# The age at which a unit's gate matmuls enter the program order: from over 13 to over 17

## The chip, the cores and the metric

The kernel runs on one core of one Trainium2 chip. The metric is the device time of one execution in microseconds (us). A core has TensorE (matmuls; the profile calls it PE, and PEld for its weight loads), VectorE (DVE), ScalarE (ACT), GpSimd (POOL, which here only issues indirect DMAs after the first few hundred microseconds) and SyncE (SP, which issues the other DMAs). Each engine works through its own instructions in the order of the program and waits on semaphores for the others.

## The reference

A causal convolution with 7 taps, whose taps are a softmax over each head's weights, makes 28672 tokens of 192 values. A gate then picks two of eight experts for each token, and the output is the weighted sum of the two experts' results:

```python
logits = x @ w_gate
noise_scale = np.log1p(np.exp(x @ w_noise))
noisy_logits = logits + noise_scale * noise
top2 = np.argpartition(-noisy_logits, 2, axis=1)[:, :2]
...                                   # top2_w: softmax over the two
for e in range(E):
    h = np.maximum(x[mask] @ w1[e], 0.0)          # 192 -> 1024
    out[mask] += top2_w[mask, k, None] * (h @ w2[e])   # 1024 -> 192
```

Here E = 8, and mask holds the tokens that have expert e as their k-th choice.

## The kernel before

**Two streams of work.** The tokens are cut into 28 units of 1024 (128 partitions by 8). A unit is convolved on DVE (`conv`, lines L411, L413: 56 instructions), scaled and split into two f16 halves in one of two buffers `rb` (ACT at L443 and L444, then DVE at L446 and L448), routed (`gating`), and its rows are written to a table `xs` in DRAM, ordered by expert (`scatter`, L567: 16 indirect DMAs on POOL for a unit). The experts work on that table in 29 rounds of 8 blocks, one block for each expert; a block has 256 rows of the table (128 in round 0). Round r, from round 9 on, needs the rows of unit r + 1 and all before it; rounds 0 to 8 need unit r.

**A block.** `load_block` loads a block's rows transposed (`bT`, SP, L688), two blocks ahead, into one of three buffers. `mm1` (L654) runs the first matrix in two halves of 20 matmuls; after each half ACT takes the ReLU (L657) and DVE what f16 left of it (L658). `mm2` (L668) runs the second matrix, 48 matmuls, one block late; ACT scales the two results (L671), and POOL adds them to the output with two indirect DMAs (L672). The order on PE is: first half of block n, `mm2` of block n-1, second half of block n. At the first block of a round SP also loads the rows' tokens and weights (`mt`, L594), and DVE makes the round's indices of them (`round_meta`, L613 to L634).

**Slots.** After each half of a block's first matrix the order has a slot: slot 2n after the first half of block n (k = 0), slot 2n + 1 after the second (k = 1). In a slot `Side.slot` first lets `pace` put one or more scatters into POOL's order, then `route` may put in some steps of one unit's routing, and then `convolve` puts in convolution work while a credit lasts. The order on PE, DVE, ACT and SP is that of the program.

**Routing of a unit** has these steps. The *first part* (age set to 0) issues on SP the unit's noise load, a store of zeros to the output and eight DMA transposes of `rb` into `xT` (L472; for units from 3 on). The *second step* puts in the 40 gate matmuls (L481), the reading of their result (L496 to L498) and an exponential (L500). Then come, each in a later slot with k = 0, log1p (L502 to L512) and the choice of two (L519 to L533), and at the next k = 1 the ranks (PE, L538 and L541), the rows' places (L545 to L563), and the 16 scatters join the queue that `pace` empties. Only now counts the unit as routed (`gate_done`).

**What couples them.** Each slot with 256 rows adds 4.05 to the age and 5.0 (k = 0) or 1.4 (k = 1) to the convolution's credit, times a rate of 0.7 where two more units are routed than the next five rounds need, or 1.0. Routing steps take from the same credit (4.1 for log1p, 3.1 for the choice, 2.8 for the places). A unit's convolution starts only when the unit two before it is routed; with it go the copy of the halo (ACT, L373) and the load of the next unit's input (L179). The ACT instruction that writes `rb` for unit u is put in once the queue holds no scatter of unit u - 2, and when it runs it waits for those scatters' DMAs to have read the buffer:

```python
while queue and queue[0][0] <= u - NRB:
    yield 0.0, True
rb = rbs[u % NRB]
nc.scalar.activation(rb[:, :, 0:128], xc[:, :, 0:128], AF.Copy)
```

`pace` takes 2 and 1 scatters in turn at each slot, or more where the round that needs them is near.

Of the kernel before, what the change touches and what calls it, by code (L numbers as in the profile page):

```python
# [32 lines left out]
def kernel(  # L33
# [305 lines left out]
    NRB, NPE = 2, 3  # L339
    rbs = []  # L340
    for i in range(NRB):
        rb = rpool.tile([P, TU, ROW], F16, name=f"rb{i}")
        V.memset(rb[:, :, 384:ROW], 0.0)
        rbs.append(rb)
    NPART = U // 2 if U % 2 == 0 else U
    nzt, route, cps = {}, {}, {}
    scat, zeroed = {}, []

# [396 lines left out]
    class Side:  # L745
# [11 lines left out]
        def route(self, k):  # L757
            if self.b is None:
                if self.gate_u <= self.conv_done and self.gate_u < U:
                    self.b, self.step, self.age = gating(self.gate_u), 0, 0.0  # L760
                    self.run_b(1)
            elif self.step == 1:
                if k == 0 and self.age > (4.0 if self.gate_u < NPE else 13.0):
                    self.run_b(3)
            elif self.step < 4:
                if k == 0:
                    self.run_b(1)
            elif k == 1:
                self.run_b(3)
                self.b = None  # L770
                self.gate_done = self.gate_u
                self.gate_u += 1
# [156 lines left out]
```

## Time and profile before

| | |
|---|---|
| three executions, median (lowest, highest) | 2248.9 us (2246.77, 2252.76) |
| the profiled execution, its own time | 2245.47 us |
| its span, first to last instruction | 2243.1 us |
| mean granted TensorE clock | 0.965 |
| PE / PEld / DVE / ACT / POOL busy, share of the span | 92% / 85% / 68% / 35% / 60% |

All numbers of the trace are of the one profiled execution. Its own time is 2.4 us above its span and 3.4 us below the median. In a listing of instructions a row has the start and the length in us, the engine, the line, the operation, what it writes and reads, and in brackets the idle time of the engine before it and what ended it. A row of a table by stretches has the bounds and the length in us, then the busy time and number of instructions of PE, PEld, DVE, ACT and POOL, the granted clock of TensorE (1.00 is full), the DMA engines' share and GB/s. A row of the waits reads "who <- what it waited for: us in total, times, longest".

### The profile page before, as it was taken

How to read it: one execution, taken by the hardware profiler on the slowest of the kernel's cores; microseconds unless marked ns; L12 is line 12 of the kernel's file. 1: busy time of each engine (PE TensorE's matmuls, PEld its weight loads, DVE VectorE, ACT ScalarE, POOL GpSimd, SP SyncE). 2: the span in 40 equal slices, each digit the busy share in tenths (PEclk: the TensorE clock that was granted, in tenths of full speed). 3: DMA queues.
4: the chain of work that ended last, by engine and by line, in shares of the span. 5: the costliest groups of instructions: out<-in, count | busy, mean ns of one | idle time of the engine just before them, and what ended most of it. 6: DMA issues, size and time to landing. Idle time of an engine off the chain costs nothing.

```text
span 2243.1 us, 53253 instructions
## 1 busy us (share of the span) xinstructions
PE 2059.7 (92%) x22126; PEld 1915.9 (85%) x22126; DVE 1523.4 (68%) x4009; ACT 795.1 (35%) x1168; POOL 1336.4 (60%) x923
## 2 busy tenths in 40 slices
PE   6569686999799999999999999999999999999997
PEld 5568585889698888899999989999999999999997
DVE  6468674788687878777778777787778875423332
ACT  5354231333233333333333333333333333333332
POOL 0463544676675676677666766667666666543333
PEclk8789797999999999999999999999999999999999
DMA  8524454565556657656556665666655665443332
GB/s 232 169 55 71 99 84 101 109 107 109 111 104 105 108 98 110 115 117 117 91 90 110 118 111 84 101 112 119 119 86 97 106 108 102 70 58 50 51 50 32
DMA packets 462774, 223.66 MB, mean 100 GB/s; under 512 B 342152, under 2 KB 449720, under 8 KB 462393
## 3 DMA queue, kind: packets, MB, share of 16 engines
q1 hardware_dynamic: 375352, 129.38, 28.6%
q0 software_dynamic: 87168, 90.76, 26.6%
q8 instruction: 175, 2.87, 0.5%
q14 instruction: 79, 0.65, 0.1%
HBM read 40.12 MB, written 115.38 MB: 69 GB/s over the span
## 4 chain that ended last, share of the span: by engine, by line
PE 68%; DVE 7%; SPq 5%; issue 4%; DMA 3%; another core or an unknown queue 3%; ACT 2%; POOL 1%; POOLq 0%; DVEq 0%; ACTq 0%
PE ph L654 34%; PE py L668 33%; SPq L472 5%; DVE h L658 3%; ACT h L657 2%; DMA xT<-rb 1%; DVE xc L413 1%; PE misc L481 1%; DMA bT<-xs 1%; POOL out_dram L672 1%; DMA out_dram<-y,ids 1%; POOL xs L567 1%; DVE xc L411 1%; ACT y L671 0%
## 5 line engine op out<-in xcount | busy, mean ns | idle before, releaser
L672 POOL DMA_INDIRECT out_dram<-y,ids x456 | 792.9, 1739 | 553.9 <-ACT y L671 338.8
L654 PE MATMUL ph<-bT,w1s 128*128 128x256 f16 (+1 forms) x9280 | 1054.8, 272 | 35.6 <-issue 17.2
L668 PE MATMUL py<-w2s,h 128*128 128x192 f16 x10944 | 976.1, 249 | 58.1 <-DVE h L658 21.5
L654 PEld LDWEIGHTS <-w1s 128*128 128x128 f16 x9280 | 893.5, 98 | 144.8 <-issue 27.8
L668 PEld LDWEIGHTS <-h 128*128 128x128 f16 x10944 | 921.8, 99 | 84.1 <-issue 43.4
L658 DVE SCALAR_TENSOR_TENSOR h<-ph,h 128x1024 f16<-128x1024 f32 (+1 forms) x464 | 557.3, 1201 | 564.8 <-ACT h L657 515.6
L567 POOL DMA_INDIRECT xs<-rb,idx x448 | 525.6, 1173 | 268.9 <-issue 187.8
L657 ACT ACTIVATE h<-ph 128x1024 f16<-128x1024 f32 (+1 forms) x464 | 466.7, 1007 | 606.6 <-PE ph L654 494.3
L413 DVE SCALAR_TENSOR_TENSOR xc<-xt,wt,xc 128x192 f32<-128x192 f32 x1248 | 426.6, 408 | 0.2 <-DMA xt<-zero 0.2
L671 ACT ACTIVATE y<-py,ga 128x192 f32<-128x192 f32 x456 | 190.1, 419 | 632.7 <-PE py L668 465.4
L411 DVE TENSOR_SCALAR xc<-xt,wt 128x192 f32<-128x192 f32 x208 | 54.0, 323 | 4.3 <-DMA xt<-in_x_dram 4.3
L481 PEld LDWEIGHTS <-xT 128*128 128x128 f16 x1120 | 34.4, 97 | 20.4 <-DMA xT<-rb 15.0
L481 PE MATMUL misc<-ghi,xT 128*128 128x16 f16 x672 | 35.4, 170 | 17.2 <-DMA xT<-rb 13.0
L508 DVE SCALAR_TENSOR_TENSOR t<-t,t 128x64 f32<-128x64 f32 x168 | 43.5, 259 | 5.8
L391 PE MATMUL ph<-xt,dg 128*128 128x192 f32 x168 | 32.8, 361 | 14.6 <-ACT dg L381 12.2
L423 DVE TENSOR_REDUCE am<-xc 128x8 f32<-128x1536 f32 (+1 forms) x27 | 45.6, 1688 | 0.3
L438 DVE TENSOR_TENSOR xc<-xc,xs 128x1536 f32<-128x1536 f32 (+1 forms) x27 | 45.7, 1691 | 0.0
L391 PEld LDWEIGHTS ph<-xt,dg 128*128 128x128 f32 x168 | 31.5, 215 | 14.7 <-ACT dg L381 12.2
L443 ACT ACTIVATE rb<-xc 128x1024 f16<-128x1024 f32 x28 | 29.4, 1051 | 38.5 <-DMA xs<-rb,idx 17.0
L283 POOL TENSOR_TENSOR w1s<-w1s,w1s 128x1024 f16<-128x1024 f32 x5 | 10.6, 2126 | 49.0 <-ACT w1s L329 46.5
L500 ACT ACTIVATE t<-t 128x64 f32<-128x64 f32 x28 | 7.2, 256 | 88.5 <-DVE t L498 76.2
L496 DVE SCALAR_TENSOR_TENSOR z<-misc,ginv,xi 128x64 f32<-128x64 f32 x28 | 7.7, 274 | 40.7 <-PE misc L481 36.1
(144 smaller groups left out, 709.4 us busy)
## 6 DMA issues: line engine op xcount, KB each, us to landing
out_dram<-zero SPq DMA_DIRECT2D x28, 768.0 KB
xt<-in_x_dram SPq DMA_DIRECT2D x27, 768.0 KB
out_dram<-y,ids POOLq DMA_INDIRECT x456
xs<-rb,idx POOLq DMA_INDIRECT x448
w2s<-in_moe_w_dram SPq DMA_DIRECT2D x16, 384.0 KB
w1s<-in_moe_w_dram SPq DMA_DIRECT2D x8, 512.0 KB
w1s<-in_moe_w_dram SPq DMA_DIRECT2D x16, 256.0 KB
bT<-xs SPq DMA_TRANSPOSE x232
```

Of the source, the lines that this page charges most:

```text
L391: nc.tensor.matmul(cps[u][-1][1][:, n % nh, :TU * G].rearrange("p (t g) -> p t g", g=G), diag[h, k], xts[u][:, k:k + TU, h * G:(h + 1) * G ...
L411: V.tensor_scalar(dst, src, wt[:, h, k:k + 1], None, op0=OP.mult)
L413: V.scalar_tensor_tensor(dst, src, wt[:, h, k:k + 1], dst, op0=OP.mult, op1=OP.add)
L472: nc.sync.dma_start(xT[:, t], rb[:, t, 0:384], transpose=True)
L481: nc.tensor.matmul(lg[:, t], xT[:, t, c, :], g[:, gc], start=(i == 0), stop=(i == len(seq) - 1))
L567: s = nc.gpsimd.indirect_dma_start(out=xsf, out_offset=bass.IndirectOffsetOnAxis(ap=idx[:, k, t:t + 1], axis=0), in_=rbf[:, t, :], in_offs ...
L654: nc.tensor.matmul(ph[:, f, :T], w1_part(e, wc, lo, half * nf + f), xT[:, c, :T], start=(i == 0), stop=(i == len(seq) - 1))
L657: halves.append(nc.scalar.activation(hh[:, hs, :T], ph[:, :, :T], AF.Relu))
L658: V.scalar_tensor_tensor(hl[:, hs, :T], ph[:, :, :T], 0.0, hh[:, hs, :T], op0=OP.max, op1=OP.subtract)
L668: nc.tensor.matmul(py[:, :D], a[:, f, ts], w2_part(e, lo, f), start=(n == 0), stop=(n == 3 * FC - 1))
L671: nc.scalar.activation(y, py[:, :D], AF.Copy, scale=gate[:, h:h + 1])
L672: a = nc.gpsimd.indirect_dma_start(out=out, out_offset=bass.IndirectOffsetOnAxis(ap=ids[:, h:h + 1], axis=0), in_=y, in_offset=None, compu ...
```

## The change

The age that a unit from unit 3 on must have passed before its second step enters the order goes from 13.0 to 17.0 (units below 3 keep 4.0):

```diff
--- before.py
+++ after.py
@@ -760,7 +760,7 @@
                     self.b, self.step, self.age = gating(self.gate_u), 0, 0.0
                     self.run_b(1)
             elif self.step == 1:
-                if k == 0 and self.age > (4.0 if self.gate_u < NPE else 13.0):
+                if k == 0 and self.age > (4.0 if self.gate_u < NPE else 17.0):
                     self.run_b(3)
             elif self.step < 4:
                 if k == 0:
```

No instruction is added or removed.

## Prediction

> **What bounds the kernel now.** I read the page, then the stages, then the waits of PE.
>
> ```profile
> span 2243.1 us, 53253 instructions
> PE 2059.7 (92%) x22126; PEld 1915.9 (85%) x22126; DVE 1523.4 (68%) x4009; ACT 795.1 (35%) x1168; POOL 1336.4 (60%) x923
> 600.00:900.00 300.00, 280.50 (x3012) 257.86 (x3011) 242.79 (x662) 100.64 (x149) 208.81 (x144) 0.98 0.63 110
> 1200.00:1500.00 300.00, 293.04 (x3236) 275.32 (x3234) 231.27 (x614) 108.69 (x158) 204.66 (x135) 0.99 0.61 103
> 383.38:391.71 8.33, 8.33 (x90) 7.88 (x88) 7.85 (x24) 2.89 (x4) 3.12 (x2) 1.00 0.36 49
> PE misc L481 <- DMA xT<-rb: 13.0, 11, 2.8
> PE misc L481 <- DMA xT<-rb: 5.6, 6, 1.7
> ```
>
> PE bounds it: from 1200 to 1500 us it idles 7 of 300 us. A block without a wait takes 8.33 us, so what counts is what a block takes beyond that. The last two rows are the wait that the change aims at, gate matmuls waiting for the eight transposes: 13.0 us in the whole span, 5.6 of them from 1000 to 1900 us. The most that can be won is small.
>
> **What moves.** Ages: a slot adds 4.05, and the second step is only taken at k = 0. If the first part came at k = 0, the ages at the next k = 0 are 8.1, 16.2, 24.3: the second step came after 4 slots and now comes after 6. If it came at k = 1 they are 4.05, 12.15, 20.25: after 5 slots in both. So only units that start at k = 0 are held back, but the credit not spent on routing goes to the convolution, which then ends earlier. I carried the planner's counters (credit, age, queue, units routed) through all 232 blocks with both thresholds:
>
> ```
>                         before                         after
> unit u   scatters of u-2  rb of u   scatters of u-2  rb of u
>    7        68 - 74          77        68 - 74         75
>    8        82 - 90          90        80 - 88         88
>    9        94 - 103        105        92 - 102       102
>   10       104 - 114        118       104 - 114       114
>   11       118 - 128        128       118 - 128       128
>   12       132 - 138        144       130 - 138       139
>   13       142 - 151        153       144 - 152       152
>   14       158 - 167        171       156 - 166       168
> each later unit, slot of a round of 16: first part 14, second step 2, routed 7, rb 10
>                                  after: first part 10, second step 0, routed 5, rb 6
> ```
>
> Order is identical up to slot 48. In steady state the convolution and transposes come two blocks earlier and the gate matmuls one block earlier; between them lie three blocks instead of two.
>
> **Term 1, steady state: -13.1 us.**
>
> ```profile
> 1607.43 13.32 SPq L472 DMA_TRANSPOSE xT<-rb  x8
> 1553.60:1622.40 68.80, 68.00 (x758) 64.13 (x755) 52.91 (x141) 25.29 (x38) 47.74 (x32) 1.00 0.61 107
> 1062.80:1901.50 838.70, 822.70 (x9041) 773.06 (x9039) 632.61 (x1663) 305.41 (x443) 568.65 (x385) 1.00 0.61 104
> 1133.00:1138.00 5.00, 5.00 (x46) 4.86 (x45) 5.00 (x17) 0.68 (x2) 4.39 (x3) 0.71 0.66 99
> 1062.97 3.98 PE py L668 x48
> 1132.51 5.63 PE py L668 x48
> ```
>
> SP spends 13.32 us on the eight transposes, and two blocks are 16.66 us, so the gate matmuls come just as the last one lands. A round without such a wait took 68.80 us; the twelve from 1062.8 to 1901.5 us took 838.70, which is 838.70 - 12 x 68.80 = 13.1 us more. The waits are only 5.6 of that; after them the clock is down to 0.71 and the next second matrix takes 5.63 instead of 3.98 us. With 25 us between, all of it goes. I take 13.1; the idle time alone is the low end.
>
> The Trainium skill ("TensorE: Matmul & The Clock Gate", section "HAM oscillation — how this bites in real kernels") says that only idle gaps over some 3.4 us throttle the clock. By it the short waits would cost their own length, this term would be near -5.6 and the sum below 7.5 us higher. The trace disagrees: 0.71 stands after waits of at most 1.7 us.
>
> **Term 2, unit 9: -6.9 us.**
>
> ```profile
> 556.97 0.17 PE L481 MATMUL misc<-ghi,xT 128*128 128x16 f16 x1
> 557.95 0.17 PE L481 MATMUL misc<-glo,xT 128*128 128x16 f16 x1
> 669.50:694.20 24.70, 21.44 (x218) 19.25 (x216) 17.50 (x51) 6.03 (x9) 16.12 (x13) 0.86 0.80 131
> ```
>
> Its gate matmuls stay at slot 112, its transposes go from slot 108 to 106. These two blocks take 24.70 - 2 x 8.33 = 8.0 us more than two blocks; 1.15 of that are the 40 matmuls themselves (the two rows are the first and last of unit 7's, which did not wait). At worst 3 us of it stays (clock).
>
> **Term 3, unit 4: -1.5 us.**
>
> ```profile
> 362.00:372.00 10.00, 2.57 (x42) 1.85 (x40) 3.49 (x6) 1.02 (x1) 1.35 (x1) 0.79 0.64 123
> 369.81 38.05 SPq L688 DMA_TRANSPOSE bT<-xs  x6
> 437.67 1.01 POOL L567 DMA_INDIRECT xs<-rb,idx  x1 [0.30 <-issue]
> 440.21 1.01 SPq L594 DMA_DIRECT2D mt<-xs  x2
> 446.33 3.92 PE L654 MATMUL ph<-bT,w1s 128*128 128x256 f16 x19 [3.08 <-DMA bT<-xs]
> ```
>
> The largest single wait: PE is busy 2.57 of 10 us at unit 4's gate matmuls. At slot 50 they wait no more, but the next block's rows are issued at 369.81, behind the transposes, and land some 5 us later (as at 446.33, from 441.2), so at most 6 of the 7.4 us are won. And unit 4's scatters now start at slot 56 instead of 54: 8.3 us later in the order, 2 to 3 by the clock. Round 4's `mt` (440.21) waits for the last scatter (437.67), and PE for what follows (446.33). So most of the 6 us come back at 446: -6 to +2, I take -1.5.
>
> **Term 4, the buffer `rb`: +23.5 us.** This speaks against the change.
>
> ```profile
> 535.34 0.99 POOL L567 DMA_INDIRECT xs<-rb,idx  x1 [0.34 <-issue]
> 581.62 0.98 POOL L567 DMA_INDIRECT xs<-rb,idx  x1 [0.30 <-issue]
> 566.56 1.02 ACT L657 ACTIVATE h<-ph 128x1024 f16<-128x1024 f32 x1 [0.30 <-PE ph L654]
> 584.60 1.06 ACT L443 ACTIVATE rb<-xc 128x1024 f16<-128x1024 f32 x1 [17.02 <-DMA xs<-rb,idx]
> 586.54 5.80 PE L668 MATMUL py<-w2s,h 128*128 128x192 f16 x48 [11.48 <-ACT y L671]
> 765.42 1.06 ACT L443 ACTIVATE rb<-xc 128x1024 f16<-128x1024 f32 x1 [5.74 <-DVE ns L512]
> 882.56 1.06 ACT L443 ACTIVATE rb<-xc 128x1024 f16<-128x1024 f32 x1 [2.99 <-DMA bT<-xs]
> 1587.10:1604.80 17.70, 16.90 (x179) 15.77 (x178) 6.39 (x7) 7.91 (x11) 14.35 (x12) 1.00 0.52 84
> 566.30:597.34 31.04, 18.96 (x187) 17.01 (x185) 14.96 (x41) 7.01 (x11) 19.57 (x15) 0.84 0.50 66
> 756.62:778.10 21.48, 17.73 (x187) 15.82 (x185) 15.58 (x44) 7.00 (x11) 12.28 (x8) 1.00 0.41 67
> 880.53:902.17 21.64, 18.72 (x188) 17.38 (x185) 13.06 (x38) 7.12 (x11) 9.41 (x6) 0.92 0.46 56
> ```
>
> POOL needs 535.34 to 582.6 = 47 us for the 16 scatters of a unit and the adds between. ACT waits for the last of them, and behind ACT wait the ReLUs and results that PE needs. Unit 8's `rb` came 8 slots after the first scatter: ACT waited 17.0 us, and the two blocks took 31.04 - 17.70 (the same two blocks in a quiet round) = 13.3 us too long. Unit 11, 10 slots: 5.7 us, cost 21.48 - 17.70 = 3.8. Unit 13, 11 slots: 3.0 us, cost 3.9 (its DVE then had log1p ahead of what PE needed). PE itself has one whole block in hand (8.33 us, two PSUM buffers), so a wait much below that costs little. After the change the distances are 10 (units 9, 10), 9 (unit 12), 8 (unit 13, before 11) and, for unit 7, 7 where they were 9:
>
> ```profile
> 471.83 0.99 POOL L567 DMA_INDIRECT xs<-rb,idx  x1 [1.61 <-DVE idx L563]
> 509.15 0.96 POOL L567 DMA_INDIRECT xs<-rb,idx  x1 [0.30 <-issue]
> 495.55 4.12 PE L668 MATMUL py<-w2s,h 128*128 128x192 f16 x48
> 513.51 1.05 ACT L443 ACTIVATE rb<-xc 128x1024 f16<-128x1024 f32 x1
> ```
>
> Unit 7's write (513.51) came just behind the last scatter (509.15 + 1, and 2 for its DMA). One block earlier, after the second half of the block whose `mm2` began at 495.55, it stands at about 502 (495.55 and 6.2 for `mm2` and half a first matrix) and waits 10 us: between 3.8 and 13.3, I take 6. Unit 9: 2.5 (between 0 and 3.8, since two gate and rank steps lie in its ten slots); unit 10: 4; unit 12: 5 (between 0 and 13.3); unit 13: 6 (13.3 less 3.9 is 9.4, but two of unit 8's POOL instructions took over 4 us, so its 17 us is high). Sum 23.5; all low 10, all high 34. Units 8 and 11 keep their distance: 0. From unit 14 on it is 12 slots or more: 0.
>
> **Term 5, SP's queue in steady state: +1.5 us.**
>
> ```profile
> 1605.10 0.34 SPq L179 DMA_DIRECT2D xt<-in_x_dram  x1
> 1620.85 17.44 SPq L688 DMA_TRANSPOSE bT<-xs  x4
> 1607.66 0.19 DVE L620 COPY_PREDICATED idf<-ok,mt 128x16 f32<-128x16 int32 x1
> 444.07 0.19 DVE L620 COPY_PREDICATED idf<-ok,mt 128x16 f32<-128x16 int32 x1 [4.71 <-DMA mt<-xs]
> ```
>
> Input load, zeros and transposes go one behind the other on SP (1605.10 to 1620.75), and the next block's rows behind them. Now they stand at slot 10, ahead of the next round's `mt` and first block (slot 12). The transposes would end some 16.0 us after slot 10's row on PE, which is 7.7 after slot 12's; `mt` takes 1.0 to issue and, by 441.2 to 444.07, 2.9 to land: 11.6 after slot 12, 3.3 after slot 14. DVE reads it 1607.66 - 1604.8 = 2.9 after slot 14, so it waits 0.4 us, which its idle time covers. The block's rows, issued 8.8 us after slot 12 and landing in about 5 (441.2 to 446.33), are needed when PE comes to its first half, 8.33 + 6.2 = 14.5 after: 0.7 us in hand. If that cover is gone, PE waits about 1 us in each of 13 rounds. Between 0 and 13, I take 1.5.
>
> **Sum.** -13.1 - 6.9 - 1.5 + 23.5 + 1.5 = +3.5 on the profiled execution's 2245.5 us: 2249.0. That execution lies 3.4 us below the median, so for the median 2248.9 + 3.5 = 2252.
>
> **Rivals.** A measurement here tells 0.3%, 6.7 us, from no change.
> 1. *Faster: `rb`'s waits stay inside PE's block in hand.* Place: ACT L443, units 7 to 13. It decides if those waits stay below some 8 us, as unit 11's 5.7. For it: 17 us was measured once, with slow POOL instructions; against: 8 and 9 slots are 33 and 37 us for 47 us of POOL work. Then the term is 10, the sum -10: 2239.
> 2. *Slower: units 7, 12 and 13 all behave like unit 8.* Term 4 near its top, 34: +14, 2263. For it: the distances 7 to 9 stand on both sides of unit 8's 8.
> 3. *Slower: the wait moves to the rows of a round's first block* (SP, L688), term 5 at 13: +15, 2264. Against: 0.7 us in hand.
> 4. *Slower: short waits never cost clock*, so term 1 is -5.6: +11, 2260. This is the rule of the Trainium skill's page named above; the 0.71 speaks against it.
> That the order does not change is excluded by the ages 16.2 and 24.3.
>
> **Chances.** My forecast, within 0.3%: 0.41. Rival 1: 0.22. Rivals 2, 3, 4: 0.22, 0.10, 0.05. So faster 0.22, same 0.41, slower 0.37. The low end, 2238, is term 4 at its 10, and 1 us for the runs' spread; the high end, 2270, is term 4 at its 34 with term 5 near 9. I leave out about 1 in 10 on each side. The forecast's own range is 2243 to 2255.
>
> **What would show it.** Right: no idle time of PE at L481 from 1000 us on and rounds near 68.8 us there; ACT waits at L443 at units 7, 9, 10, 12 and 13, with PE idle at L668 behind them. Wrong: ACT waits of under 5 us there; `mt` or L654 waiting for SP in every round; rounds that stay at 69.9 us.

## The result

The change made the kernel slower: 2269.9 us median (2269.55 to 2272.14) against 2247.8 (2235.53 to 2252.76) for the kernel before, ratio 1.0109 with a 95% interval of 1.0067 to 1.0150. 2252 was forecast, within a range of 2238 to 2270. The likeliest case, no difference that can be told, did not come: the interval lies wholly above 1.

The page of the changed kernel, span and engines:

```profile
span 2270.1 us, 53244 instructions
PE 2065.4 (91%) x22126; PEld 1907.7 (84%) x22126; DVE 1524.6 (67%) x4009; ACT 793.4 (35%) x1168; POOL 1297.0 (57%) x923
```

The span is 27.0 us longer, PE's busy time only 5.7 us. So the loss is for the most part idle time of PE.

To find where it lies I cut both executions at the same three matmuls, the first of `mm2` at slots 42, 174 and 402. The first stretch ("ramp") holds units 4 to 13, the second ("steady state") the rounds that all look alike; each holds the same matmuls in both kernels. After slot 402 hardly any block differs from 8.33 us in either. Columns of this view: from:to, length, then busy us (count) of PE, PE's weight loads, DVE, ACT, POOL, then the granted clock, the DMA share and GB/s. Before:

```profile
319.50:974.84 655.34, 592.53 (x6310) 541.50 (x6307) 505.24 (x1392) 215.53 (x316) 428.19 (x299) 0.96 0.58 105
974.84:1969.96 995.12, 976.40 (x10721) 917.15 (x10719) 730.25 (x1929) 360.28 (x523) 674.46 (x460) 1.00 0.60 104
```

After:

```profile
320.64:988.74 668.10, 594.84 (x6310) 538.98 (x6307) 509.51 (x1406) 215.43 (x316) 438.89 (x299) 0.95 0.56 104
988.74:1997.95 1009.21, 979.76 (x10720) 911.28 (x10718) 728.13 (x1915) 358.65 (x522) 628.38 (x462) 1.00 0.59 101
```

Ramp: +12.8 us, forecast +15.1 (terms 2, 3 and 4). Steady state: +14.1 us, forecast -11.6 (terms 1 and 5). The steady state is 25.7 us above its forecast, the ramp 2.3 below. That the ramp's sum fits so well is luck: term 3 was about 10 us too low and term 4 about 14 too high (see below).

The waits for `rb` came where term 4 put them. The writes of units 7, 8, 12 and 13 on ACT after the change, the wait in brackets; those of units 9, 10 and 11 waited 5.0, 6.5 and 3.4 us (the profile puts unit 7's down to the DMA of an add; the last scatter of unit 5 ended at 518.4 us, some 3.5 us ahead of the write):

```profile
521.89 1.06 ACT L443 ACTIVATE rb<-xc 128x1024 f16<-128x1024 f32 x1 [8.09 <-DMA out_dram<-y,ids]
589.08 1.06 ACT L443 ACTIVATE rb<-xc 128x1024 f16<-128x1024 f32 x1 [11.13 <-DMA xs<-rb,idx]
828.71 1.06 ACT L443 ACTIVATE rb<-xc 128x1024 f16<-128x1024 f32 x1 [8.39 <-DMA xs<-rb,idx]
896.65 1.06 ACT L443 ACTIVATE rb<-xc 128x1024 f16<-128x1024 f32 x1 [10.09 <-DMA xs<-rb,idx]
```

And PE stands behind them. Its first row here is unit 4's turn: the gate matmuls wait no more, the next block's rows do. The others follow the writes of units 7, 12 and 13:

```profile
377.64 1.67 PE L654 MATMUL ph<-bT,w1s 128*128 128x256 f16 x7 [7.86 <-DMA bT<-xs]
525.69 3.94 PE L654 MATMUL ph<-bT,w1s 128*128 128x256 f16 x20 [5.31 <-DVE h L658]
832.51 3.78 PE L654 MATMUL ph<-bT,w1s 128*128 128x256 f16 x18 [4.92 <-DVE h L658]
898.59 3.63 PE L668 MATMUL py<-w2s,h 128*128 128x192 f16 x20 [4.60 <-ACT y L671]
```

In the steady state the wait that the change aims at has gone, as forecast, and others are there. PE's groups from 1050 to 1900 us; behind the bar busy us, mean ns, then the idle time before them and what ended it. Before:

```profile
L668 PE MATMUL py<-w2s,h 128*128 128x192 f16 x4656 | 405.2, 247 | 8.2 <-DVE h L658 8.2
L481 PE MATMUL misc<-ghi,xT 128*128 128x16 f16 x288 | 15.3, 170 | 6.9 <-DMA xT<-rb 5.6 <-issue 1.0
```

After:

```profile
L654 PE MATMUL ph<-bT,w1s 128*128 128x256 f16 x3820 | 437.3, 273 | 6.0 <-DMA bT<-xs 3.3 <-issue 2.4
L668 PE MATMUL py<-w2s,h 128*128 128x192 f16 x4608 | 403.5, 246 | 19.6 <-DVE h L658 14.6 <-issue 4.1 <-ACT h L657 0.3
L481 PE MATMUL misc<-ghi,xT 128*128 128x16 f16 x288 | 13.5, 169 | 0.0
```

L481: 6.9 us of idle time before, none after. But PE now idles 19.6 us ahead of `mm2` (8.2 before), mostly for DVE's half of `h`, and 6.0 us ahead of the first matrix, 3.3 of them for rows (`bT`). What DVE waits for is ACT, and what ACT waits for is shown as "remote", a release that no instruction of this profile explains. ACT's waits from 1050 to 1900 us, total, times, longest, before:

```profile
ACT y L671 <- remote: 50.1, 16, 3.4
ACT h L657 <- remote: 36.9, 12, 3.2
```

After:

```profile
ACT h L657 <- remote: 55.8, 20, 3.3
ACT y L671 <- remote: 41.8, 14, 3.7
```

A late `y` (L671) ends none of PE's idle time there; a late `h` holds up DVE and then PE, and of these there are 20 in place of 12.

### The profile page after: what moved, and what is told of

The parts are those of the page before. It is cut to its first block, busy times and chain, and to the rows that moved or that the text cites. A ratio compares the mean times of both kernels' runs of the same rounds, so it can differ in the third digit from the quotient of the medians.

```text
span 2270.1 us, 53244 instructions
## 1 busy us (share of the span) xinstructions
PE 2065.4 (91%) x22126; PEld 1907.7 (84%) x22126; DVE 1524.6 (67%) x4009; ACT 793.4 (35%) x1168; POOL 1297.0 (57%) x923
## 3 DMA queue, kind: packets, MB, share of 16 engines
q1 hardware_dynamic: 375352, 129.38, 27.7%
## 4 chain that ended last, share of the span: by engine, by line
PE 60%; DVE 13%; issue 5%; POOL 4%; DMA 4%; another core or an unknown queue 3%; ACT 3%; SPq 2%; POOLq 0%; ACTq 0%; DVEq 0%
PE ph L654 29%; PE py L668 29%; DVE h L658 5%; POOL xs L567 3%; DVE xc L413 2%; ACT h L657 2%; DMA out_dram<-y,ids 2%; SPq L472 1%; DMA bT<-xs 1%; POOL out_dram L672 1%; PE misc L481 1%; DVE t L508 1%; DVE am L423 1%; DMA xs<-rb,idx 1%
## 5 line engine op out<-in xcount | busy, mean ns | idle before, releaser
L668 PE MATMUL py<-w2s,h 128*128 128x192 f16 x10944 | 976.7, 248 | 75.1 <-issue 34.5
L668 PEld LDWEIGHTS <-h 128*128 128x128 f16 x10944 | 913.8, 99 | 109.7 <-issue 63.3
L658 DVE SCALAR_TENSOR_TENSOR h<-ph,h 128x1024 f16<-128x1024 f32 (+1 forms) x464 | 557.8, 1202 | 590.0 <-ACT h L657 532.8
L567 POOL DMA_INDIRECT xs<-rb,idx x448 | 492.4, 1099 | 301.7 <-issue 118.2
L671 ACT ACTIVATE y<-py,ga 128x192 f32<-128x192 f32 x456 | 190.0, 419 | 632.8 <-PE py L668 451.9
L391 PEld LDWEIGHTS ph<-xt,dg 128*128 128x128 f32 x168 | 31.5, 215 | 15.3 <-ACT dg L381 12.8
L446 DVE TENSOR_TENSOR rb<-xc,rb 128x1024 f16<-128x1024 f32 x28 | 34.1, 1218 | 1.5 <-issue 0.8
L481 PEld LDWEIGHTS <-xT 128*128 128x128 f16 x1120 | 32.7, 96 | 1.3 <-ACT xT L464 0.5
L620 DVE COPY_PREDICATED idf<-ok,mt 128x16 f32<-128x16 int32 (+1 forms) x29 | 5.6, 193 | 40.4 <-DMA mt<-xs 34.6
L481 PE MATMUL misc<-ghi,xT 128*128 128x16 f16 x672 | 32.0, 170 | 0.4 <-ACT xT L464 0.4
```

The lines of the kernel that those rows point to most:

```text
L391: nc.tensor.matmul(cps[u][-1][1][:, n % nh, :TU * G].rearrange("p (t g) -> p t g", g=G), diag[h, k], xts[u][:, k:k + TU, h * G:(h + 1) * G ...
L481: nc.tensor.matmul(lg[:, t], xT[:, t, c, :], g[:, gc], start=(i == 0), stop=(i == len(seq) - 1))
L567: s = nc.gpsimd.indirect_dma_start(out=xsf, out_offset=bass.IndirectOffsetOnAxis(ap=idx[:, k, t:t + 1], axis=0), in_=rbf[:, t, :], in_offs ...
L658: V.scalar_tensor_tensor(hl[:, hs, :T], ph[:, :, :T], 0.0, hh[:, hs, :T], op0=OP.max, op1=OP.subtract)
L668: nc.tensor.matmul(py[:, :D], a[:, f, ts], w2_part(e, lo, f), start=(n == 0), stop=(n == 3 * FC - 1))
L671: nc.scalar.activation(y, py[:, :D], AF.Copy, scale=gate[:, h:h + 1])
```

## Experiments

They ran on chips 14, 9 and 6, where the kernel before takes 2208 to 2211 us and not 2248, which is why both kernels were run again (second experiment). Which chip the first pair ran on is not recorded. By its times I take it to be another one and call it the first chip; that the chip and nothing else of that session makes the difference is not shown. Ratios are always to the kernel before on the same chip. My theory after the traces: the ramp's loss is `rb`'s, the steady state's is a second, separate one. Rivals: all is the ramp's; or what happens in the steady state is the chip's and not the program's.

This table has the stretches of all profiles, cut as above (us; one profile of each; the rows of the profiles that the verdicts rest on follow). Where two of them hold the same ramp ("before" and "17 from unit 14 on", "after" and "17 up to unit 13") they agree within 1.0 us:

```
                                          ramp 42-174   steady 174-402   ratio to before (95%)
before, first chip                           655.3          995.1
after, first chip                            668.1         1009.2        1.0109 (1.0067-1.0150)
before                                       643.0          977.0
after                                        662.2          979.5        1.0090 (1.0069-1.0112)
17 from unit 14 on                           643.7          977.9        1.0005 (0.9990-1.0021)
17, unit 4 with 13                           675.1          977.6        1.0160 (1.0140-1.0180)
17, rb two slots behind                      635.0          974.4        0.9949 (0.9933-0.9966)
17, two scatters in a slot                   674.0          971.0        1.0142 (1.0123-1.0161)
17 up to unit 13                             661.2         1042.8        1.0354 (1.0333-1.0375)
13, rb two slots behind                      640.6         1032.4        1.0215 (1.0191-1.0239)
17, rb four slots behind                     642.6          973.8        0.9988 (0.9970-1.0006)
17, rb two behind, transposes spread         630.3          971.2        0.9925 (0.9901-0.9950)
17, rb four behind, two scatters             643.1          974.2        1.0003 (0.9989-1.0017)
```

**The steady state alone.**

```
-                if k == 0 and self.age > (4.0 if self.gate_u < NPE else 17.0):
+                if k == 0 and self.age > (4.0 if self.gate_u < NPE else 17.0 if self.gate_u > 13 else 13.0):
```

> Bound 13 for the units up to 13, 17 from unit 14 on: the ramp is that of before, the steady state (units 14 to 27) has the logits one block later. Between the two profiles the later kernel loses 14 us between slots 176 and 398, where it was forecast to gain 13. Theory A (the steady state is slower by itself: in the new place another wait, of TensorE for VectorE's h, comes more often than the wait it replaces): about 14 us above before, 2262. Theory B (the steady state gains as forecast and the slot count only inherits something from the ramp, such as a shifted phase of the rounds): 13 us below before, 2235. Theory C (neither matters, the whole loss is in the ramp): 2248.

2210.8 us against 2208.2, ratio 1.0005: theory C. On this chip the later logits cost the steady state nothing on balance and bring it nothing.

**Both kernels on one chip.** No edit.

> The kernel before, unchanged, profiled on one chip with the next three, since the first chip showed waits of ScalarE at L657 and L671 that it puts down to a remote releaser (37 and 50 us of them between 1050 and 1950 us before the change, 56 and 42 after it), and the next chip none. Theory A (those late releases are the chip's and not the program's): without them a steady round takes about 69 us whether the logits come at slot 2 or at slot 0, TensorE's slots 174 to 402 last 975 to 980 us as in the run with bound 17 from unit 14 on (978). Theory B (the place of the logits counts also there): the wait of the gate matmuls costs the 13 us forecast, and these slots last about 990 us. With late releases as on the first chip: 995.

> The changed kernel, unchanged, on the same chip. Theory A (the ramp's waits at L443 are the loss, the steady state is the chip's matter): 20 to 35 us above the kernel before, ratio 1.009 to 1.016, all of it before slot 176, and slots 174 to 402 equal to those of the kernel before within 5 us. Theory B (half the loss is the steady state's): the ramp costs about 14 us and slots 174 to 402 another 14.

The kernel before, 2213.2 us:

```profile
318.85:961.86 643.01, 579.32 (x6309) 540.67 (x6307) 504.19 (x1392) 216.51 (x316) 437.75 (x299) 0.96 0.58 107
961.86:1938.82 976.96, 970.62 (x10720) 917.30 (x10718) 730.73 (x1929) 363.97 (x523) 644.14 (x461) 1.00 0.61 106
```

The changed kernel, 2232.5 us, ratio 1.0090:

```profile
318.44:980.66 662.22, 585.16 (x6310) 542.91 (x6308) 508.87 (x1406) 215.82 (x316) 440.92 (x299) 0.95 0.56 105
980.66:1960.13 979.47, 971.11 (x10720) 913.64 (x10718) 728.63 (x1915) 363.02 (x522) 632.44 (x462) 1.00 0.61 104
```

Theory A. The total loss is as on the first chip, 21 us, but now 19.2 of it lie in the ramp and 2.5 in the steady state. No wait of ACT is put down to a remote releaser in either kernel; ACT waits for PE's matmuls themselves.

So most of the 14 us of the steady state are seen only where the late releases are seen. These seem to cost the kernel before as well: its steady state took 995.1 us there and 977.0 here.

What has become of the wait that the change removes? PE's groups from 1050 to 1750 us, before:

```profile
L654 PE MATMUL ph<-bT,w1s 128*128 128x256 f16 x3254 | 370.2, 273 | 0.0
L481 PE MATMUL misc<-ghi,xT 128*128 128x16 f16 x240 | 13.1, 170 | 5.3 <-DMA xT<-rb 5.1
```

After:

```profile
L654 PE MATMUL ph<-bT,w1s 128*128 128x256 f16 x3247 | 370.6, 273 | 5.1 <-DMA bT<-xs 5.1
L481 PE MATMUL misc<-ghi,xT 128*128 128x16 f16 x264 | 12.4, 169 | 0.0
```

5.1 us for `xT` have turned into 5.1 us for `bT`. The mean length of a block by its slot in the round (from the first matmul of `mm2` to the next block's, slots 178 to 370; what is put in at a slot counts to the block before it) shows it in place:

```
slot of the round        0      2      4      6      8     10     12     14    round
before, first chip   10.12   8.63   8.33   8.56   8.33   8.33   9.16   8.45   69.90
after, first chip     8.58   8.33   8.91   8.35   8.33   9.27   8.91  10.26   70.93
before                9.95   8.45   8.33   8.58   8.33   8.33   8.33   8.33   68.61
after                 8.32   8.33   8.89   8.35   8.33   8.33   8.33   9.85   68.72
17 up to unit 13     10.22   8.33   8.56   8.33   8.33   8.33   8.33  13.29   73.71
```

The gate matmuls have gone from the block of slot 0 to that of slot 14, which takes 9.85 us where that of slot 0 took 9.95. The ranks have gone from the block of slot 6 to that of slot 4 and lengthen it by 0.56 us where they cost 0.25. On the first chip blocks of slots 10 to 14 wait for DVE's `h` as well.

**The ramp alone.**

```
+  ... else 13.0 if self.gate_u > 13 else 17.0):
```

> Bound 17 up to unit 13, 13 from unit 14 on: the ramp of the changed kernel (the same program up to slot 172), and a steady state whose logits lie at slot 0, rb copies at slot 9. Theory A (the loss is the ramp's): as slow as the changed kernel within 5 us. Theory B (half is the steady state's at bound 17): 14 us faster than the changed kernel.

The ramp, 661.2 us, is that of the changed kernel (662.2), so its loss does not hang on the steady state. But the total was 2290.4, ratio 1.0354, which neither theory has. The steady state falls into a third phase: first part at slot 12, logits at slot 0.

```profile
315.88:977.08 661.20, 584.55 (x6310) 542.31 (x6308) 508.38 (x1406) 216.09 (x316) 440.11 (x299) 0.95 0.56 105
977.08:2019.88 1042.80, 998.80 (x10720) 940.10 (x10718) 732.14 (x1915) 364.67 (x522) 615.48 (x462) 0.97 0.58 98
```

Four slots lie between first part and logits, as in the kernel before, but there the transposes start 14.0 us ahead of the first gate matmul and here 10.2. The kernel before, SyncE's queue and PE:

```profile
1445.56 14.49 SPq L472 DMA_TRANSPOSE xT<-rb  x8
1459.55 0.17 PE L481 MATMUL misc<-ghi,xT 128*128 128x16 f16 x1
```

This kernel, then its group of gate matmuls from 1050 to 1750 us:

```profile
1492.90 12.32 SPq L472 DMA_TRANSPOSE xT<-rb  x8
1503.11 0.17 PE L481 MATMUL misc<-ghi,xT 128*128 128x16 f16 x1
L481 PE MATMUL misc<-ghi,xT 128*128 128x16 f16 x240 | 16.5, 173 | 37.5 <-DMA xT<-rb 37.3
```

Here the wait is worth something: 37.5 us in ten rounds, and it costs clock. Against the changed kernel on the same chip PE idles 35.6 us more in the steady state (44.0 against 8.4) and is busy 27.7 us longer with the same matmuls (998.8 against 971.1), at a granted clock of 0.97 in place of 1.00.

**The write of `rb` two slots behind the scatters.** `last[u]` holds the slot of the unit's last scatter, `tick` counts slots.

```
-        while queue and queue[0][0] <= u - NRB:
+        while (queue and queue[0][0] <= u - NRB) or last.get(u - NRB, -9) + 2 > tick[0]:
```

> Bound 17, and the copies into a unit's rb wait in the order of the program until two slots after the last scatter of the unit two before, so that ScalarE finds the buffer free. The seven waits at L443 (8.1, 11.1, 5.0, 6.5, 3.4, 8.4 and 10.1 us after the change) go. Theory A (these waits are what TensorE's idle times of about 7 us at unit 7, 6 at unit 8, 6.5 at unit 12 and 4.6 at unit 13 come from): slot 176 comes some 20 us earlier, total about 2250. Theory B (the units then come late by as much, or DMA and VectorE fill the gap): 2265 to 2270. The slower steady state stays in both (+14 us of slots 176 to 398).

2198.1 us, ratio 0.9949: faster than the kernel before by 10 us and, by the ratios, than the changed one by 31. The ramp is 27.2 us shorter than in the changed kernel on chip 9:

```profile
315.89:950.89 635.00, 578.61 (x6310) 539.83 (x6308) 506.64 (x1392) 216.52 (x316) 433.88 (x292) 0.96 0.58 107
950.89:1925.27 974.38, 970.61 (x10720) 913.96 (x10718) 732.82 (x1929) 362.90 (x523) 638.94 (x468) 1.00 0.63 107
```

Theory A, and more than its 20, though the waits at the write are only eased. What ended ACT's idle time ahead of the write, 440 to 1000 us, in the changed kernel (total, times):

```profile
  DMA xs<-rb,idx: 60.2, 6
```

and with the later write, to 1010 us:

```profile
  DMA xs<-rb,idx: 38.9, 6
```

The waits of units 9 to 12 are gone but for 0.5 us; those of units 7 (10.7 us), 8 (4.2), 13 (10.7), 14 (7.0) and 15 (5.8) are left. What counts is what PE waits for. Its waits for `y` and `h` from 330 to 1000 us, in the changed kernel:

```profile
PE py L668 <- ACT y L671: 17.5, 5, 6.4
PE ph L654 <- DVE h L658: 14.1, 2, 9.2
PE py L668 <- DVE h L658: 5.6, 6, 1.7
```

and with the later write (the added lines move L668, L671 and L658 to L670, L673 and L660):

```profile
PE py L670 <- ACT y L673: 11.7, 3, 5.1
PE py L670 <- DVE h L660: 0.9, 1, 0.9
```

That is 37.2 us against 12.6: 24.6 of the 27.2.

**The same at bound 13.** The edit of the last one, with 13.

> Bound 13 as before, and the copies into rb two slots behind the last scatter of the unit two before. The kernel before waits 17, 6 and 3 us at L443 in units 8, 11 and 13. Theory A (these waits cost before as well, and the later logits gain nothing by themselves): about as fast as bound 17 with the later copies, ratio to before 0.993 to 0.997. Theory B (with the waits out of the way the later logits gain their 21 us of gate-matmul waits, as forecast): 0.5 to 1% slower than bound 17 with the later copies, so 1.000 to 1.005 of before.

2260.1 us, ratio 1.0215: neither, since its steady state falls into the third phase too (1032.4 us). The ramp answers by itself: 640.6 us, 2.4 less than before, against 635.0 with bound 17. So with the waits for `rb` eased the later logits seem to gain in the ramp, 5.6 us, as far as one profile of each on two chips can tell.

**Unit 4 as before.**

```
+  ... else 13.0 if self.gate_u == 4 else 17.0):
```

> Bound 17 for all units but unit 4, which keeps 13. In the profile of the changed kernel the block of slot 58 took 25.7 us instead of 10.2 while GpSimd issued unit 4's 16 scatters nearly back to back; 5.3 us of it came back later through a wait for bT that was gone. Theory A (that stall comes from unit 4's late scatters): it goes, TensorE's slot 64 comes about 10 us earlier, total 2260 against 2270 (ratio to before about 1.005). Theory B (the stall belongs to the place in the program, not to the scatters): it stays, 2270. Under both the L443 waits of units 7, 10, 12, 13 and the slower rounds stay.

2246.0 us, ratio 1.0160: both theories missed. From slot 42 to 66, where unit 4 counts, it takes 139.7 us (before 139.0, after 145.2), so the later unit 4 costs the changed kernel 5.5 us there. The stall of the block of slot 58 did not occur on these chips in any kernel, so it tells nothing of its cause. The loss is further on: with unit 4 earlier units 7 to 13 stand at distances of 7, 8, 9, 10, 10, 7 and 8 slots, and ACT waits longer ahead of the write, at unit 9 14.1 us in place of 6.6 and at unit 12 12.7 in place of 8.4; in all:

```profile
  DMA xs<-rb,idx: 73.7, 6
```

**Two scatters in every slot.**

```
-                issue(max(1 + self.now % 2, -(-n // max(left, 1))))
+                issue(max(2, -(-n // max(left, 1))))
```

> Bound 17, and two scatters in every slot in place of one and two in turn: a unit's 16 scatters take 8 slots, not 11, and end three slots earlier (in a steady round slots 6 to 13 in place of 6 to 16). Theory A (TensorE is late for as long as GpSimd scatters, whatever the density; fewer slots, fewer late blocks; and the L443 waits of the ramp go): 25 us below the changed kernel in the ramp and at least a part of the 14 us of the steady state, 2235 to 2248. Theory B (it is the density of the scatters that makes TensorE's blocks late, as in the 25.7 us block of unit 4's scatters): the ramp gains, each steady round loses, 2250 to 2275. Theory C (the scatters have nothing to do with the steady state): 2246, and rounds as long as in the changed kernel, about 70.9 us.

2238.7 us, ratio 1.0142: none of the three, the ramp loses where A and B had it gain. The steady state is the shortest of all (971.0 us), so denser scatters do not hold up PE there; the ramp is nearly the worst (674.0). In the order of the program the scatters now take 8 slots, some 33 us, but GpSimd took 37 to 43 for those of units 5 to 10, and waits of 3.3 to 13.9 us at the write of units 7 to 12 stayed. GpSimd itself runs behind the order.

**Four slots behind.**

```
+  ... or last.get(u - NRB, -9) + 4 > tick[0]:
```

> Bound 17, the copies into rb four slots behind the last scatter of the unit two before, not two. With two slots waits at L443 stayed in units 7 (11.1 us), 8 (4.7), 13 (11.1), 14 (7.5) and 15 (6.3), since GpSimd runs some two slots behind the order of the program; TensorE idled 5.1 us at units 7 and 13 and 1.4 at unit 14 for them. Theory A (each of these waits costs what TensorE idles at it): 10 to 14 us below the version with two slots, ratio to before about 0.989. Theory B (the later copies make the units late, and waits for bT, 12.9 us at 446 and 6.3 at 806 in the version with two slots, grow by as much): 0.995 or above.

2206.5 us, ratio 0.9988: theory B. The waits for `rb` are all but gone (2.2 us in one), but that brings no more, since PE now waits for rows of units that come too late:

```profile
448.51 1.89 PE L656 MATMUL ph<-bT,w1s 128*128 128x256 f16 x8 [12.88 <-DMA bT<-xs]
813.28 2.10 PE L656 MATMUL ph<-bT,w1s 128*128 128x256 f16 x9 [11.48 <-DMA bT<-xs]
```

**Both together,** four slots behind and two scatters in a slot.

> Bound 17, copies four slots behind, and two scatters in every slot. Two in every slot made the steady round 0.5 us shorter (68.21 us against 68.72), but the ramp was slow by waits at L443 of 3.7 to 14.4 us in units 7 to 12. Theory A (those waits were all that was wrong with it): 7 us below the version with copies four slots behind and one and two scatters in turn. Theory B (denser scatters hold up the adds on GpSimd and so y, in the ramp above all): no faster than that version.

2209.5 us, ratio 1.0003: theory B, and the 0.5 us a round are not there either (68.54 us).

**Transposes spread,** with the write two slots behind. `transposes(n)` issues up to n of those that are left; the last ones go out ahead of the gate matmuls.

```
-            for t in range(TU):
-                nc.sync.dma_start(xT[:, t], rb[:, t, 0:384], transpose=True)
+            trans.extend(functools.partial(nc.sync.dma_start, xT[:, t], rb[:, t, 0:384], transpose=True)
+                         for t in range(TU))
+            transposes(2)
...
             tick[0] += 1
+            transposes(2)
```

> Bound 17, copies two slots behind, and a unit's eight transposes spread over four slots, two in each, in place of all eight in one. In the changed kernel TensorE waits for a bT in the steady rounds (5.1 us in 1050 to 1750, where the kernel before waited 5.1 us for xT and nothing for bT): that block's load stands behind the eight transposes on SyncE's queue. Theory A (the wait for xT has only changed into one for bT through this queue): the bT waits go, 0.4 to 0.6 us for each of 14 rounds, 5 to 8 us in all, ratio to before about 0.992. Theory B (the load is late by the DMA engines' share, not by its place in the queue): nothing, 0.995; a new wait at the gate matmuls would show the transposes come too late.

2193.9 us, ratio 0.9925, the fastest. From 1050 to 1750 us PE waits for neither `bT` nor `xT` (with all eight in one slot it waited 1.6 us for `bT`); the steady state is 3.2 us shorter than with all eight in one slot (971.2 against 974.4), the round 0.27 us. That is theory A with about half of its size; the intervals of the totals of these two versions overlap, so the step is read from the stretches alone. At one place PE now waits for `xT`, where two transposes stand on SyncE's queue behind round 4's `mt`, which waits for scatters: 16.6 us, up to 442.84. That is no loss on balance: from slot 42 to 66 this version takes 142.7 us and the one with all eight in one slot 142.6.

## Why the prediction was wrong

- **The step that failed is the price of the new place: term 5 (+1.5) was too small, and the steady state's other blocks were put at nothing without a reason.** Terms 1 and 5 together were -11.6; measured were +14.1 on the first chip and +2.5 on chip 9, where both kernels were run again. A block whose gate matmuls wait for nothing took 9.33 us at a clock of 1.00 (first chip, before, from 1613.08 us), 1.00 more than a plain one. With it the table by slots gives, in us for a round:

```
blocks of                                      forecast   first chip   chip 9
slots 0, 2: gate matmuls gone, without their 1.00   -1.09        -0.84    -0.75
slot 14: gate matmuls come, without their 1.00      +0.12        +0.81    +0.52
slots 4, 6: the ranks, one block earlier             0           +0.37    +0.33
slots 8, 10, 12                                      0           +0.69     0.00
```

- **Term 1** (-13.1, -1.09 a round) came for the larger part: from unit 3 on PE has no idle time at L481, and the slow matmuls behind it went as well. Its sum was sound: in its twelve rounds the blocks of slots 0 and 2 alone are 12.8 us longer than in the quiet round. These rounds also hold waits for `h`, 8.2 us from 1050 to 1900, but the quiet round of 68.80 us has its own, so they drop out of the difference:

```profile
1597.58 2.98 PE L668 MATMUL py<-w2s,h 128*128 128x192 f16 x34 [0.80 <-DVE h L658]
```

- **Term 5** (+1.5, between 0 and 13) named the queue that then showed it, loads behind eight transposes on SyncE, but trusted in 0.7 us in hand. On chip 9 PE waited 5.1 us for `bT` in ten rounds, so the wait for `xT` changed into one for `bT` of the same length: rival 3 at half its size. Spreading the transposes took that kind of wait away. On the first chip waits for `h`, and idle time for which the profile has no releaser, came on top at slot 14.
- **What had no term.** In the blocks of slots 4 and 6 only 0.6 us in ten rounds is a wait that the profile names (PE at L538 for DVE's L533, on chip 9); the rest stays open. In slots 8 to 12 PE waits for `h` behind late releases of ACT, on the first chip alone. So "rounds near 68.8 us" was wrong there (70.93) and right on chip 9 (68.72), where they were at 68.61 before.
- That short waits cost clock, which rival 4 denied, held. The run with 17 up to unit 13 shows it at size: 35.6 us of idle time more, 27.7 us of matmuls more. The Trainium skill's rule in "TensorE: Matmul & The Clock Gate" (section "HAM oscillation — how this bites in real kernels") is "no PE-idle gaps >~3.4µs"; that only such gaps count is the prediction's reading of it, and shorter ones cost clock here. Two waits of one group of gate matmuls stand 0.3 us apart, 4.0 us together, and whether the rule would take them as one gap no run here tells:

```profile
1505.24 0.18 PE L481 MATMUL misc<-ghi,xT 128*128 128x16 f16 x1 [1.13 <-DMA xT<-rb]
1508.39 0.20 PE L481 MATMUL misc<-ghi,xT 128*128 128x16 f16 x1 [2.87 <-DMA xT<-rb]
```

  All waits of PE at the gate matmuls of that run from 1050 to 1900 us, total, times, longest:

```profile
PE misc L481 <- DMA xT<-rb: 40.7, 35, 2.9
```

- **Term 3** (-1.5, between -6 and +2) had the mechanism and not the size. From slot 42 to 66 the change cost 8.7 us on the first chip (139.0 to 147.7) and 6.1 on chip 9 (139.0 to 145.2). Of "at most 6 of the 7.4 us" that slot 50 was to win, 1.6 us came on the first chip and nothing on chip 9: the wait went over to the next block's rows. Then round 4's first rows came later. On chip 9, PE's wait for them before the change and, in the second fence, after it:

```profile
445.52 4.19 PE L654 MATMUL ph<-bT,w1s 128*128 128x256 f16 x20 [6.12 <-DVE xc L413]
```

```profile
450.65 1.68 PE L654 MATMUL ph<-bT,w1s 128*128 128x256 f16 x7 [12.64 <-DMA bT<-xs]
```

  On the first chip the block of slot 58 stalled instead, 10.7 us of work in 20 at a clock of 0.68 (416 to 436 us), with no releaser in the profile.

- **Term 2** (-6.9): from slot 108 to 114, unit 9's place, 4.9 us less on the first chip and 5.4 on chip 9. Right in kind, a little too large.
- **Term 4** (+23.5): ACT waits at every unit named. From slot 66 to 174 the change cost 4.0 us on the first chip and 13.1 on chip 9; with term 2's gain taken out, 9 and 18. On the first chip the blocks around the writes of units 7 and 12 (slots 74 to 82, 138 to 148) grew by 8.4 and 8.5 us (forecast 6 and 5), but those around unit 13's (150 to 170) by only 0.4 (forecast 6), and units 8 and 11 (86 to 98, 126 to 138), put at 0, gave 6.1 and 6.4 back: unit 8's wait went from 17.0 to 11.1 us. With the write two slots later the ramp is 27.2 us shorter, so this term is the larger part of the loss on the later chips, and the loss can be avoided. A third buffer, with the write left where it stands, was not run.
- The range held the time only just (2269.9 of 2270), and that is luck too: on the first chip the steady state's 25.7 us and term 3's 10 too little stood against term 4's 14 too much.

## What to carry to other kernels

A wait that goes is half of the sum. List, block by block, what the moved steps find at their new place (the queue, the engine that reads their result, the engine that shares it) and give each a term: here the old place gave 0.8 us a round and the new ones took 0.9 to 1.9. When a step moves later, look at who frees the buffer that the next step writes, and move that write along: with it the same change is 0.5% faster than before, without it 0.9% slower. A planner's threshold also picks the phase in which its steady state settles; in the two runs that fell into the third phase that decided more (58 and 62 us) than the move itself.

## What was not expected of the hardware

- The kernel before took 2248 us in the first pair and 2208 to 2211 on three other chips. 18 us of that are the steady state, where only the first pair shows releases of ACT with no releaser in the profile (87 us from 1050 to 1900 before, 98 after, none elsewhere). Their cause stays open: no later run shows them. That they make up what the changed kernel lost there beyond the others' 2.5 us is argued from the waits and from their absence elsewhere, and not shown by an experiment.
- Two scatters in every slot raise their rate by less than the order does. In the order a unit's sixteen take 8 slots in place of 11; from the first to the last 35.7 us passed in the steady state (unit 24, 1712.0 to 1747.8 us), against 40.9 with one and two in turn (1709.2 to 1750.1 in the changed kernel).
- Waits of at most 2.9 us, several in a row among small matmuls, went with 0.8 us of slower matmuls for each us of idle time (27.7 us for 35.6, granted clock 0.97).
